# One level of Strassen's algorithm in the second product of five batches

## The chip, the core and the metric

The kernel runs on one core of a Trainium2 chip. TensorE (PE) multiplies; VectorE (DVE), ScalarE (ACT) and GpSimd (POOL) do the elementwise work; SyncE (SP) and the POOL queue issue transfers. The metric is device time in microseconds from a launch on the chip.

## The reference

```python
scores = scale * x @ state.T                  # per batch and head: 512 x 32
a = softmax(scores, -1);   xread = a @ state
scores2 = scale * state @ x.T                 # 32 x 512
a2 = softmax(scores2, -1); sread = a2 @ x
t = concat([xread, sread], axis=2)            # (8, 8, 544, 64)
x2 = t.transpose(0, 2, 1, 3).reshape(4352, 512)
h = x2 @ w_in                                 # 512 -> 2048
g = max(h, 0) + alpha * min(h, 0)
out = g @ w_out                               # 2048 -> 512, float32
```

There are 8 batches of 8 heads, each with 512 tokens and 32 states of width 64. The rows of a batch are its 512 token reads, then its 32 state reads.

## The kernel before

**Stages.** For a batch `b` of token rows, the state times `w_in` is formed first (`state_w_in`, step `m`, and its copy out of PSUM, `mo`), so that the first product needs only the softmax weights: `first` (step `F.b.jc.k`) multiplies the weights of two groups of four heads with `m`, 2 matmuls of 512 columns for each of the 16 blocks `jc` of 128 hidden units. The result `h` (128 hidden units x 512 tokens) lies in PSUM bank `k`. `negative` (step `N`, ACT) writes relu(-h) as float32 to SBUF, and `prelu` (step `G`, DVE), called the gate below, adds it, scaled by 1 - alpha, to `h` and writes `gt` in float16. `second` (step `S.b.q.jc2`) multiplies the gates with `w_out`: for each of 4 token tiles `q`, 16 matmuls of 128 x 128 weights and 512 columns accumulate in one PSUM bank, two to a step. `second_out` (step `O`, ACT or DVE) copies the bank to SBUF and stores it from the SP queue.

**Softmax.** A batch's scores (`sc`) serve both softmaxes. For the token reads: block transpose on DVE (`sb`), maximum (`smax`, DVE), subtraction (`ssh`, here called the shift, POOL), exponential (`sexp`, ACT), sum and reciprocal (`ssum`, DVE), multiplication (`snorm`, the state norm, POOL) and transpose back (`wb`, DVE). For the state reads: maximum and its scaling (`tm`, DVE), exponential (`te`, ACT), reciprocal (`tsum`, DVE), multiplication (`tn`, the token norm, POOL, in place on 128 x 512 float16), a transposing transfer (`tt`, SP queue), 32 narrow matmuls (`rd`) and a cast into `XS` (`rdo`). The state reads of all batches form a ninth batch of 256 rows (`F.8`, `R`, `RO`). The tokens of a batch are loaded from the POOL queue (`lx`) and transposed by a transfer of the SP queue (`xd`).

**Order.** Every step is a token of the text `ORDER` (lines 17 to 102), written out by hand or by a planner, and the kernel issues the steps in that order; each engine takes its own in order, and waits follow from the data and from the buffers. Eight PSUM banks serve everything: a pair `two` for scores and state products and six single ones, whose number is the last part of a token such as `F.2.3.0`. So a first product can go on only when a gate has freed its bank. `L` and `LO` are the last token tile of batch 7 in three pieces of 256, 128 and 128 columns. SBUF buffers with one tag are used in turn: `gt` 2 per block, `neg` 4, `osb` 4, `m` 7.

Of the kernel before, what the change touches and what calls it, by code (L numbers as in the profile page):

```python
# [12 lines left out]
ALU = mybir.AluOpType  # L13
# [28 lines left out]
mo.3.1.a.0 mo.2.2.a.0 S.1.2.7 S.1.0.0.3 mo.3.1.a.1 F.2.3.0 O.1.2.a S.1.0.1 N.2.3 smax.3 F.2.12.5  # L42
N.2.12 G.2.3 F.2.4.2 N.2.4 G.2.12 F.2.2.1 S.1.1.7 F.2.15.0 S.1.0.2 O.1.1.a tm.3 S.1.3.0.5 F.2.0.4
N.2.15 ssh.p.3 S.1.0.3 G.2.4 S.1.3.1 S.1.0.4 F.2.1.2 S.1.3.2 N.2.2 G.2.2 N.2.0 G.2.15 sexp.3 F.2.9.1
G.2.0 S.1.3.3 tsum.2 F.2.6.0 S.1.0.5 N.2.1 G.2.1 S.1.0.6 F.2.13.4 ssum.3 S.1.3.4 N.2.9 te.3.1
F.2.11.2 te.3.0 S.1.3.5 S.1.3.6 N.2.6 G.2.9 G.2.6 F.2.5.1 N.2.13 S.1.3.7 G.2.13 S.1.0.7 N.2.11
G.2.11 N.2.5 O.1.3.a tn.2.0 O.1.0.a F.2.7.0 rd.1.4 G.2.5 m.4.3.2.5 sc.4 m.3.3.1.3 tsum.3 rdo.1.a
mo.4.3.a.1 snorm.p.3 mo.3.3.a.1 wb.3 tn.2.1 N.2.7 mo.3.3.v.0 S.2.1.0.4 lx.5 mo.4.3.v.0 F.3.4.5 G.2.7
S.2.1.1 F.2.8.3 F.2.10.1 N.3.4 S.2.1.2 N.2.8 G.3.4 tt.2 F.3.6.2 N.2.10 G.2.8 G.2.10 F.3.8.0
S.2.0.0.5 N.3.8 F.3.7.3 N.3.6 S.2.1.3 S.2.1.4 N.3.7 F.3.9.1 S.2.0.1 N.3.9 S.2.1.5 tn.3.0 sb.4 tn.3.1  # L50
G.3.7 G.3.8 G.3.9 F.2.14.3 S.2.0.2 S.2.1.6 F.3.13.0 S.2.0.3 F.3.14.1 smax.4 xd.5 S.2.0.4 G.3.6
N.2.14 S.2.0.5 G.2.14 S.2.3.0.2 S.2.3.1 F.3.2.3 S.2.3.2 N.3.14 S.2.3.3 tm.4 N.3.13 S.2.0.6 ssh.p.4
G.3.14 S.2.3.4 S.2.0.7 F.3.1.1 G.3.13 F.3.3.0 sexp.4 te.4.1 ssum.4 te.4.0 N.3.2 S.2.1.7 S.2.3.5
G.3.2 S.2.3.6 tsum.4 S.2.3.7 tt.3 N.3.1 N.3.3 O.2.1.a O.2.0.a G.3.1 m.6.0 G.3.3 O.2.3.a mo.6.0.a.1
m.5.1.3.1 mo.6.0.v.0 snorm.p.4 m.4.2.4.0 rd.2.5 rd.3.2 mo.4.2.a.0 mo.5.1.a.0 rdo.3.a mo.4.2.v.1
rdo.2.v sc.5 m.4.1.4.0 m.5.0.5.3 mo.5.1.v.1 S.2.2.0.2 mo.4.1.a.0 F.3.10.1 tn.4.1 F.3.5.4 tn.4.0
mo.5.0.a.0 mo.4.1.a.1 N.3.10 tm.5 mo.5.0.a.1 S.2.2.1 F.3.11.5 S.2.2.2 F.3.0.0 S.2.2.3 wb.4 N.3.5
S.2.2.4 N.3.11 G.3.10 N.3.0 F.3.12.3 N.3.12 F.4.0.1 S.2.2.5 sb.5 G.3.5 S.2.2.6 lx.6 S.2.2.7 lx.7
te.5.0 F.4.9.4 N.4.0 te.5.1 G.3.11 G.3.12 G.3.0 tsum.5 O.2.2.a F.3.15.5 F.4.6.3 S.3.3.0.0 S.3.3.1
N.4.9 G.4.0 S.3.3.2 S.3.3.3 S.3.3.4 N.3.15 smax.5 S.3.3.5 F.4.5.2 G.3.15 G.4.9 F.4.3.1 tt.4 N.4.6  # L60
tn.5.0 tn.5.1 N.4.3 S.3.3.6 F.4.1.5 G.4.6 G.4.3 N.4.5 tt.5 S.3.0.0.4 G.4.5 S.3.0.1 F.4.4.3 N.4.4
S.3.0.2 ssh.v.5 N.4.1 F.4.2.1 S.3.3.7 S.3.0.3 S.3.0.4 O.3.3.a sexp.5 S.3.0.5 G.4.4 F.4.7.2 G.4.1
S.3.0.6 N.4.7 S.3.1.0.3 S.3.1.1 ssum.5 S.3.1.2 G.4.7 F.4.8.0 F.4.11.5 N.4.8 S.3.0.7 N.4.2 snorm.v.5
N.4.11 S.3.1.3 xd.6 S.3.1.4 S.3.1.5 O.3.0.a S.3.1.6 G.4.2 rd.4.2 G.4.8 rdo.4.a G.4.11 rd.5.1
m.5.3.4.0 rdo.5.a m.5.2.5.2 sc.6 wb.5 tm.6 mo.5.3.a.0 mo.5.2.a.1 S.3.2.0.1 S.3.2.1 F.4.10.4 N.4.10
# [40 lines left out]
def kernel(  # L106
# [47 lines left out]
    def engine(e):  # L154
        return nc.gpsimd if e == "p" else nc.vector
# [4 lines left out]
    def load_x(b):  # L160
# [10 lines left out]
    st0_32 = consts.tile([128, 2, D], F32)  # L171
    x32 = [
        moe.tile([128, 2, 2, 2, D], F32, name=f"x32_{i}", tag="osb", bufs=4) for i in range(2)
    ]
    al32 = consts.tile([32, 128], F32)
# [160 lines left out]
    def score_blocks(b, j=None):  # L336
        if j in (None, 0):
            halved.discard(b) if j is None else halved.add(b)
            live["ts", b] = att.tile([128, 2 * S], F32, name=f"ts_{b}", tag="ts", bufs=2)
            live["mx", b] = att.tile([128, 2 * S // N], F32, name=f"mx_{b}", tag="mx", bufs=2)  # L340
            live["r1", b] = att.tile([128, 2 * S // N], F32, name=f"r1_{b}", tag="r1", bufs=2)
            live["an", b] = att.tile([128, 2 * S], F16, name=f"an_{b}", tag="an", bufs=2)
            live["aT", b] = att.tile([128, 2 * S], F16, name=f"aT_{b}", tag="aT", bufs=2)
# [29 lines left out]
    def state_norm(e, b, j=None):  # L373
        engine(e).tensor_tensor(  # L374
            blocks(cols(live["an", b], j, S)),
            blocks(cols(live["ts", b], j, S)),
            over_blocks(cols(live["r1", b], j, S // N)),
            ALU.mult,
        )

    def weights_back(b, j=None):
        nc.vector.transpose(cols(live["aT", b], j, S), cols(live["an", b], j, S))  # L382
# [275 lines left out]
```

## Time and profile before

| | us |
|---|---|
| three runs | 219.62, 218.71, 219.16 |
| median | 219.16 |
| span of the profiled execution | 217.3 |
| median less span | 1.9 |
| last matmul ends | 214.3 |

The time of the profiled execution itself is not listed apart from the three; the span runs from its first to its last instruction. In the rows below a line of a group has the source line, engine, operation, output <- inputs, shapes and count, then busy time and mean length of one, then idle time before them and what ended it. A line of the timeline has start, length, engine, line, operation and count. Matmuls overlap in the pipeline, so the cost of one in a stream is read from starts, not from its length.

### The profile page before, as it was taken

How to read it: one execution, taken by the hardware profiler on the slowest of the kernel's cores; microseconds unless marked ns; L12 is line 12 of the kernel's file. 1: busy time of each engine (PE TensorE's matmuls, PEld its weight loads, DVE VectorE, ACT ScalarE, POOL GpSimd, SP SyncE). 2: the span in 40 equal slices, each digit the busy share in tenths (PEclk: the TensorE clock that was granted, in tenths of full speed). 3: DMA queues.
4: the chain of work that ended last, by engine and by line, in shares of the span. 5: the costliest groups of instructions: out<-in, count | busy, mean ns of one | idle time of the engine just before them, and what ended most of it. 6: DMA issues, size and time to landing. Idle time of an engine off the chain costs nothing.

```text
span 217.3 us, 4301 instructions
## 1 busy us (share of the span) xinstructions
PE 211.0 (97%) x1692; PEld 104.1 (48%) x1692; DVE 169.2 (78%) x260; ACT 138.0 (63%) x271; POOL 64.8 (30%) x54
## 2 busy tenths in 40 slices
PE   6989999999999999999999999999999999999994
PEld 5763344444444444444454443444455555554553
DVE  1897998899999999798898989989966566665001
ACT  3498995699888748986655768566367336544021
POOL 7589034605238813915000320902200000000000
PEclk9999999999999999999999999999999999999999
DMA  6999999599660875499460432032061011110124
GB/s 148 180 205 207 206 202 160 63 250 168 98 162 3 168 109 113 148 129 163 103 142 0 134 62 98 0 108 41 0 195 51 0 48 51 48 38 10 51 97 145
DMA packets 39316, 23.39 MB, mean 108 GB/s; under 512 B 21872, under 2 KB 35328, under 8 KB 39296
## 3 DMA queue, kind: packets, MB, share of 16 engines
q0 software_dynamic: 12176, 8.36, 26.9%
q1 hardware_dynamic: 26704, 14.43, 26.7%
q10 hardware_dynamic: 416, 0.33, 0.5%
q8 instruction: 13, 0.21, 0.4%
q14 instruction: 7, 0.06, 0.1%
HBM read 17.31 MB, written 8.91 MB: 121 GB/s over the span
## 4 chain that ended last, share of the span: by engine, by line
PE 90%; DVE 6%; DMA 1%; ACT 1%; POOL 0%; issue 0%
PE o L548 49%; PE h L496 24%; PE m_ps L463 3%; PE h L505 3%; PE o L596 3%; DVE gt L536 2%; PE sr_ps L438 2%; PE o L568 2%; DMA st<-in_state_dram 1%; PE sc L313 1%; PE z L232 1%; PE xT_ps L299 1%; DVE aT L382 1%; DVE m L485 1%; DVE r L370 1%; DVE nb L394 1%
## 5 line engine op out<-in xcount | busy, mean ns | idle before, releaser
L548 PE MATMUL o<-w_out_sb,gt 128*128 128x512 f16 x496 | 126.4, 379 | 0.1
L528 ACT ACTIVATE neg<-h 128x512 f32<-128x512 f32 (+1 forms) x144 | 77.4, 580 | 45.2 <-PE h L496 31.4
L536 DVE SCALAR_TENSOR_TENSOR gt<-neg,oma_sb,h 128x512 f16<-128x512 f32 x128 | 89.7, 736 | 15.4 <-ACT neg L528 14.6
L548 PEld LDWEIGHTS <-gt 128*128 128x128 f16 x496 | 47.3, 98 | 54.9 <-issue 3.7
L496 PE MATMUL h<-aT,m 128*128 128x512 f16 x250 | 69.2, 379 | 0.3 <-DVE gt L536 0.3
L496 PEld LDWEIGHTS <-m 128*128 128x128 f16 x250 | 24.2, 98 | 29.7 <-issue 1.6
L419 POOL TENSOR_SCALAR e<-e,r 128x512 f16<-128x512 f16 x16 | 25.0, 1568 | 25.2 <-DVE r L415 20.6
L485 ACT CAST m<-m_ps 128x512 f16<-128x512 f32 x50 | 27.9, 603 | 3.7 <-PE m_ps L463 2.0
L360 POOL TENSOR_TENSOR ts<-ts,mx 128x1024 f32<-128x1024 f32 (+1 forms) x8 | 13.6, 1698 | 43.6 <-DVE mx L354 43.6
L586 ACT COPY osb<-o 128x512 f32<-128x512 f32 x22 | 12.8, 591 | 16.4 <-PE o L548 16.4
L374 POOL TENSOR_TENSOR an<-ts,r 128x1024 f16<-128x1024 f32 (+1 forms) x7 | 11.7, 1667 | 18.1 <-DVE r L371 18.0
L405 ACT ACTIVATE e<-sc,nb 128x512 f16<-128x512 f32 x16 | 11.1, 697 | 1.5 <-issue 1.5
L463 PE MATMUL m_ps<-w_in_sb,stT 64*32 64x512 f16 x256 | 11.7, 383 | 0.1
L536 DVE SCALAR_TENSOR_TENSOR gs<-neg,oma_sb,h 128x256 f16<-128x256 f32 x16 | 7.5, 476 | 5.1 <-ACT neg L528 5.1
L370 DVE TENSOR_REDUCE r<-ts 128x32 f32<-128x1024 f32 (+1 forms) x9 | 9.8, 1093 | 1.3 <-ACT ts L366 1.3
L485 DVE CAST m<-m_ps 128x512 f16<-128x512 f32 x14 | 9.3, 684 | 1.6 <-ACT m L485 1.4
L382 DVE STREAM_TRANSPOSE aT<-an 128x1024 f16<-128x1024 f16 (+1 forms) x9 | 10.0, 1114 | 0.5 <-POOL an L374 0.4
L354 DVE TENSOR_REDUCE mx<-ts 128x32 f32<-128x1024 f32 (+1 forms) x9 | 9.9, 1096 | 0.1
L394 DVE TENSOR_REDUCE nb<-sc 128x2 f32<-128x1024 f32 x8 | 9.7, 1212 | 0.1
L232 PE MATMUL z<-zero 128*128 128x128 f16 x76 | 7.6, 263 | 1.9 <-DVE zero L226 1.1
L606 DVE COPY osr<-o 128x512 f32<-128x512 f32 x1 | 0.7, 692 | 11.3 <-PE o L596 11.3
L505 PE MATMUL h<-XS,w_in_sb 128*128 128x256 f16 x64 | 9.4, 273 | 0.0
(55 smaller groups left out, 130.9 us busy)
## 6 DMA issues: line engine op xcount, KB each, us to landing
out_dram<-osb SPq DMA_DIRECT2D x29, 256.0 KB, 2.3
xg<-in_x_dram POOLq DMA_DIRECT2D x7, 512.0 KB, 7.5
w_in_sb<-in_moe_w_in_dram POOLq DMA_DIRECT2D x4, 512.0 KB, 11.6
w_out_sb<-in_moe_w_out_dram POOLq DMA_DIRECT2D x4, 512.0 KB, 12.8
out_dram<-osb SPq DMA_DIRECT2D x5, 128.0 KB, 2.0
out_dram<-osr SPq DMA_DIRECT2D x2, 256.0 KB, 2.5
x<-in_x_dram SPq DMA_DIRECT2D x1, 256.0 KB, 3.7
x<-in_x_dram ACTq DMA_DIRECT2D x1, 256.0 KB, 3.9
```

The source lines that it names most:

```text
L360: engine(e).tensor_tensor(ts, ts, over_blocks(cols(live["mx", b], j, S // N)), ALU.subtract)
L370: nc.vector.tensor_reduce(r1, blocks(cols(live["ts", b], j, S)), AX.X, ALU.add)
L382: nc.vector.transpose(cols(live["aT", b], j, S), cols(live["an", b], j, S))
L419: nc.gpsimd.tensor_scalar_mul(e2, e2, live["r2", b][:, g : g + 1])
L463: nc.tensor.matmul(t[N * k : N * (k + 1), :], st_head(b, h)[64 * r : 64 * r + 64, :], w_in_sb[64 * r : 64 * r + 64, c, 512 * f : 512 * (f ...
L485: copier(e)(m_tile(b)[:, f, g, :], live["mp", b, f][g])
L496: nc.tensor.matmul(h.rearrange("p (r j s) -> p r j s", r=2, j=2), ms[b][:, f, g, 128 * j : 128 * (j + 1)], weights(b, g), start=(g == 0), ...
L505: nc.tensor.matmul(h, w_in_sb[:, c, 128 * jc : 128 * (jc + 1)], XS[:, c].rearrange("p q n b -> p (q n b)"), start=(c == 0), stop=(c == n_c ...
L528: nc.scalar.activation(neg, h, RELU, bias=0.0, scale=-1.0)
L536: nc.vector.scalar_tensor_tensor(gt, negs.pop((b, jc)), oma_sb[:, jc : jc + 1], h, ALU.mult, ALU.add)
L548: nc.tensor.matmul(outs[b, q], gts[b, jc][:, 128 * q : 128 * (q + 1)], w_out_sb[:, jc, :], start=(jc == 0), stop=(jc == n_jc - 1),)
L586: copier(e)(osb, t)
```

## The change

The second product of batches 2 to 6 is no longer made by `second` and `second_out`. Let A be the gates of a batch (512 tokens x 2048 hidden units) and B the matrix `w_out` (2048 x 512), each cut in 2 x 2 blocks: tokens in halves of 256, hidden units in halves of 8 blocks, output columns in halves of 256. The form with seven products and fifteen additions (Winograd's) is used:

- `weight_sum` (steps `T`, POOL, eight pieces in all): four matrices `ws` from the blocks of B, once: B12 - B11, B22 - ws0, B22 - B12, B21 - ws1.
- `token_sum_of` (steps `A.b.i.grp`, POOL, eight per batch): s1 = A21 + A22, s3 = A11 - A21, s2 = A22 - s3, s4 = A12 - s2, each in two groups of four blocks, 128 x 4 x 256 in float16.
- `product` (steps `P.b.p.c`): seven products, each of 8 blocks x 2 token tiles in matmuls of 256 columns, four to a step. Products 1, 6, 7 and 4 accumulate in one bank, 5 and 3 in a second, 2 in a third.
- `product_out` (steps `Q`): the bank of product 1 is copied behind product 1 (`p1`) and behind product 6 (`u`), product 5's behind product 5 (`p5`); c11 = p1 + product 2; c22 = p5 + the first bank behind product 7; c12 = u + the second bank behind product 3; c21 = the first bank behind product 4. Copies are on ACT (one `u` on DVE), the three additions of a batch on DVE. Each quarter, 256 tokens x 256 columns, is stored from SP.

The gates of four blocks now share a tile (`gp`, two groups, 2 buffers each), and those of the ninth batch take a buffer of tag `m`. Tags and counts change: `m` 5 buffers, `osb` 5, and some constants share `neg`. Of the softmax steps behind the cut, the token norms of batches 2 to 7 go from POOL to DVE, and the two state norms and one shift that DVE had go to POOL. Behind `mo.3.1.a.1` every step of all engines is in a new order; ahead of it none is.

```diff
@@ order, from where it differs (two stretches)
-mo.3.1.a.0 mo.2.2.a.0 S.1.2.7 S.1.0.0.3 mo.3.1.a.1 F.2.3.0 O.1.2.a S.1.0.1 N.2.3 smax.3 F.2.12.5
+mo.3.1.a.0 mo.2.2.a.0 S.1.2.7 S.1.0.0.3 mo.3.1.a.1 T.0.0.p T.0.1.p tsum.2 tm.3 rd.1.0 O.1.2.a
+S.1.0.1 rdo.1.a T.1.0.p F.2.0.2 tn.2.0.v te.3.1 tn.2.1.v S.1.0.2 smax.3 tt.2 F.2.1.5 N.2.0 S.1.0.3
...
+sb.5 F.4.2.0 mo.5.0.a.0 P.3.5.0.2 mo.5.0.a.1 F.4.3.5 tm.5 N.4.2 P.3.5.1 N.4.3 A.3.2.0.p F.4.8.1
+P.3.5.2 G.4.2 N.4.8 F.4.9.4 te.5.1 G.4.3 P.3.5.3 F.4.10.0 N.4.9 G.4.8 A.3.2.1.p P.3.6.0 Q.3.p5.a
+G.4.9 P.3.2.0.5 N.4.10 P.3.6.1 smax.5 te.5.0 F.4.11.1 lx.6 P.3.6.2 N.4.11 G.4.10 m.5.1 ssh.p.5
+P.3.6.3 mo.5.1.a.0 G.4.11 P.3.2.1 mo.5.1.a.1 tsum.5 F.4.4.4 Q.3.u.v P.3.2.2 tn.5.0.v N.4.4 A.3.4.0.p
+P.3.7.0 tn.5.1.v sexp.5 tt.5 G.4.4 P.3.2.3 F.4.5.0 Q.3.c11.v P.3.7.1 N.4.5 ssum.5 F.4.6.1 A.3.4.1.p
...
-    def token_norm(b, g):
+    def token_norm(b, g, e="p"):
         e2 = live["e2", b][:, g, :, :]
-        nc.gpsimd.tensor_scalar_mul(e2, e2, live["r2", b][:, g : g + 1])
+        r2 = live["r2", b][:, g : g + 1]
...
+            engine(e).tensor_scalar_mul(e2, e2, r2)
...
-            gt = moe.tile(list(h.shape), F16, name=f"gt_{b}_{jc}", tag=f"gt{jc}", bufs=2)
+            grp = jc % 8 // 4
+            if (b, grp) not in gps:
+                gps[b, grp] = moe.tile(
+                    [128, 2, 4, S], F16, name=f"gp_{b}_{grp}", tag=f"gp{grp}", bufs=2
+                )
+            gt = gps[b, grp][:, jc // 8, jc % 4, :]
...
+    def token_sum_of(b, i, grp, e):
+        t = sums[b, i, grp] = moe.tile(
+            [128, 4, half_s], F16, name=f"s{i}_{b}_{grp}", tag=f"s_{grp}", bufs=3
+        )
+        gp = gps[b, grp]
+        a11, a12, a21, a22 = (
+            gp[:, k, :, half_s * r : half_s * (r + 1)] for r in range(2) for k in range(2)
+        )
+        x, y, op = {
+            1: (a21, a22, ALU.add),
+            2: (a22, sums.get((b, 3, grp)), ALU.subtract),
+            3: (a11, a21, ALU.subtract),
+            4: (a12, sums.get((b, 2, grp)), ALU.subtract),
+        }[i]
+        engine(e).tensor_tensor(t, x, y, op)
+
+    chain_of = {1: 1, 6: 1, 7: 1, 4: 1, 2: 0, 5: 2, 3: 2}
+
+    def product(b, p, c, k=None):
+        chain = b, chain_of[p]
+        opens = p in (1, 2, 5)
+        if opens and c == 0:
+            chains[chain] = single(k, f"p{p}_{b}", [128, 2, half_d], F32)
+        for i in (2 * c, 2 * c + 1):
+            for t in range(2):
...
+                nc.tensor.matmul(
+                    chains[chain][:, t, :],
+                    lhs,
+                    rhs[:, i, :],
+                    start=(opens and i == 0 and t == 0),
+                    stop=(i == half_k - 1),
+                    skip_group_check=True,
+                )
...
+    def product_out(b, name, e):
+        if name in ("p1", "p5", "u"):
+            t = parts[b, name] = moe.tile(
+                [128, 2, half_d], F32, name=f"{name}_{b}", tag="osb", bufs=5
+            )
+            copier(e)(t, chains[b, 2 if name == "p5" else 1])
+            return
+        osb = moe.tile([128, 2, half_d], F32, name=f"{name}_{b}", tag="osb", bufs=5)
+        if name == "c21":
+            copier(e)(osb, chains.pop((b, 1)))
+        else:
+            chain, part = {"c11": (0, "p1"), "c12": (2, "u"), "c22": (1, "p5")}[name]
+            nc.vector.tensor_tensor(osb, parts.pop((b, part)), chains[b, chain], ALU.add)
+        nc.sync.dma_start(block_rows(b, *blocks_of[name]), osb)
```

More of the change, by code (lines that the diff above doesn't have):

```diff
@@ L170 @@
     n_j = (B * H * N - n0) // 128
-    st0_32 = consts.tile([128, 2, D], F32)
+    st0_32 = moe.tile([128, 2, D], F32, name="st0_32", tag="neg", bufs=4)
     x32 = [
-        moe.tile([128, 2, 2, 2, D], F32, name=f"x32_{i}", tag="osb", bufs=4) for i in range(2)
+        moe.tile([128, 2, 2, 2, D], F32, name=f"x32_{i}", tag="osb", bufs=5) for i in range(2)
     ]
-    al32 = consts.tile([32, 128], F32)
+    al32 = moe.tile([32, 128], F32, name="al32", tag="neg", bufs=4)
     nc.vector.memset(al32, 0.0)
@@ L373, in state_norm @@
     def state_norm(e, b, j=None):
+        if ("an", b) not in live:
+            live["an", b] = att.tile([128, 2 * S], F16, name=f"an_{b}", tag="an", bufs=2)
         engine(e).tensor_tensor(
@@ L381, in weights_back @@
     def weights_back(b, j=None):
+        if ("aT", b) not in live:
+            live["aT", b] = att.tile([128, 2 * S], F16, name=f"aT_{b}", tag="aT", bufs=2)
         nc.vector.transpose(cols(live["aT", b], j, S), cols(live["an", b], j, S))
@@ L528, in negative, with reads_tile @@
         nc.scalar.activation(neg, h, RELU, bias=0.0, scale=-1.0)
+    def reads_tile():
+        if "gs" not in live:
+            live["gs"] = moe.tile([128, n_jc, B * N], F16, name="gs", tag="m", bufs=5)
+        return live["gs"]
     def prelu(b, jc):
@@ L554, in second, with w_block, weight_sum @@
             )
+    half_k, half_d, half_s = n_jc // 2, d_model // 2, S // 2
+    ws = {}
+    sums = {}
+    chains = {}
+    parts = {}
+    def w_block(k, d):
+        return w_out_sb[:, half_k * k : half_k * (k + 1), half_d * d : half_d * (d + 1)]
+    def weight_sum(i, part, e):
+        if i not in ws:
+            ws[i] = consts.tile([128, half_k, half_d], F16, name=f"ws_{i}")
+        b11, b12, b21, b22 = (w_block(k, d) for k in range(2) for d in range(2))
+        x, y = ((b12, b11), (b22, ws.get(0)), (b22, b12), (b21, ws.get(1)))[i]
+        at = slice(4 * part, 4 * part + 4)
+        engine(e).tensor_tensor(ws[i][:, at, :], x[:, at, :], y[:, at, :], ALU.subtract)
@@ L584, in second_out @@
         t = outs.pop((b, q))
-        osb = moe.tile([128, d_model], F32, name=f"osb_{b}_{q}", tag="osb", bufs=4)
+        osb = moe.tile([128, d_model], F32, name=f"osb_{b}_{q}", tag="osb", bufs=5)
         copier(e)(osb, t)
@@ L604, in second_reads_out @@
     def second_reads_out(q, e):
-        osb = moe.tile([128, d_model], F32, name=f"osr_{q}", tag="osb", bufs=4)
+        osb = moe.tile([128, d_model], F32, name=f"osr_{q}", tag="osb", bufs=5)
         copier(e)(osb, outs.pop((B, q)))
```

146 lines of the change are left out of this document (81 added, 65 removed).

## The prediction

> **What bounds the kernel now.** I read the page first, for the busy shares and the chain that ended last.
>
> ```profile
> span 217.3 us, 4301 instructions
> PE 211.0 (97%) x1692; PEld 104.1 (48%) x1692; DVE 169.2 (78%) x260; ACT 138.0 (63%) x271; POOL 64.8 (30%) x54
> ...
> PE 90%; DVE 6%; DMA 1%; ACT 1%; POOL 0%; issue 0%
> PE o L548 49%; PE h L496 24%; PE m_ps L463 3%; PE h L505 3%; PE o L596 3%; DVE gt L536 2%; PE sr_ps L438 2%; PE o L568 2%; DMA st<-in_state_dram 1%; PE sc L313 1%; PE z L232 1%; PE xT_ps L299 1%; DVE aT L382 1%; DVE m L485 1%; DVE r L370 1%; DVE nb L394 1%
> ```
>
> TensorE (PE) carries 90% of the chain, and half of the chain is the second product, line 548, which the change rewrites for five batches. Busy shares are averages, so next I cut the span where the two orders part. That is at the matmul which opens the third batch (58.35); the second cut is at the first matmul of batch 7.
>
> ```profile
> 58.35 0.59 PE L496 MATMUL h<-aT,m 128*128 128x512 f16 x2
> ```
>
> ```profile
> 58.35:163.50 105.15, 105.15 (x856) 48.48 (x855) 95.35 (x137) 73.01 (x143) 34.76 (x22) 1.00 0.46 99
> 163.50:217.40 53.90, 50.82 (x299) 27.78 (x297) 24.32 (x43) 20.64 (x45) 0.00 (x0) 1.00 0.15 54
> ```
>
> The columns after the length are PE, weight loads, DVE (VectorE), ACT (ScalarE), POOL (GpSimd), clock, DMA share and GB/s. In the first stretch PE is busy for all of its 105.15 us at full clock, while DVE fills 95.35, ACT 73.01 and POOL 34.76. The list of PE's waits agrees: the last and only one on the elementwise work is small.
>
> ```profile
> PE h L496 <- DVE gt L536: 0.3, 1, 0.3
> ```
>
> So matmul time taken out behind 58.35 shortens the span one for one, until another engine fills its stretch. Ten microseconds of free DVE time is the smallest cushion.
>
> **The matmuls.** Pieces of the chain (start, length, count) give what one matmul costs in a stream, each with its own weight load; the first two are two state reads, 0.56 each, and one batch's scores, 0.4.
>
> ```profile
> 89.26 1.12 PE sr_ps L438 x64
> 90.38 0.41 PE sc L313 x16
> ...
> 110.40 2.16 PE o L548 x10
> ...
> 180.95 0.87 PE h L505 x8
> ...
> 213.42 0.91 PE o L568 x16
> ```
>
> A 512-column matmul costs 2.16/10 = 0.216 us, a 256-column one 0.87/8 = 0.109, a 128-column one 0.91/16 = 0.057. A batch had 64 of the first kind, 13.82 us. Seven products of 8 blocks times 2 token tiles are 112 of the second kind, 12.21 us. Five batches save 5 x 1.61 = **8.1 us**. That weight loads come twice as often costs nothing extra here, because the 128-column row already has them four times as often.
>
> The new order also splits the narrow matmuls (state times weights, scores, state reads) into more groups. Behind 58.35 I count 7 uninterrupted groups in the old order and 15 in the new. A group has an entry and an exit cost:
>
> ```profile
> 120.87 1.03 PE L496 MATMUL h<-aT,m 128*128 128x512 f16 x4
> 121.83 0.41 PE L463 MATMUL m_ps<-w_in_sb,stT 64*32 64x512 f16 x8
> 122.17 0.60 PE L548 MATMUL o<-w_out_sb,gt 128*128 128x512 f16 x2
> ...
> 130.81 0.59 PE L548 MATMUL o<-w_out_sb,gt 128*128 128x512 f16 x2
> 131.34 0.62 PE L463 MATMUL m_ps<-w_in_sb,stT 64*32 64x512 f16 x16
> 131.90 1.90 PE L548 MATMUL o<-w_out_sb,gt 128*128 128x512 f16 x8
> ```
>
> The last wide matmul before the first group starts at 120.87 + 3 x 0.216 = 121.52 and the next at 122.17: 0.65, less its own 0.216 leaves 0.43 for 8 narrow matmuls. The second group, from 131.03 to 131.90, leaves 0.65 for 16. So eight cost 0.22 and a group 0.21. Eight more groups add **1.7 us**.
>
> At the end the last three pieces are now all copied by ACT, close together, instead of one.
>
> ```profile
> 214.35 0.27 ACT L579 COPY osb<-o 128x128 f32<-128x128 f32 x1 [0.26 <-PE o L568]
> 214.64 0.33 SPq L580 DMA_DIRECT2D out_dram<-osb  x1
> ```
>
> Another such copy may stand behind the last matmul, and its store behind another store: 0 to 0.6, I take **0.3 us**.
>
> **DVE.** Up to the first matmul of batch 7 the new order gives it 3 more gates (line 536), 12 additions of a PSUM chain to an SBUF part, one PSUM copy, 12 token norms taken from POOL and 4 more state-read casts; it takes away 6 output copies, 4 casts of the state product, two state norms and one shift.
>
> ```profile
> 5.12 0.43 DVE L197 CAST xg<-x 128x512 f16<-128x512 f32 x1 [0.99 <-DMA x<-in_x_dram]
> ...
> 89.63 1.29 DVE L485 CAST m<-m_ps 128x512 f16<-128x512 f32 x2 [1.17 <-ACT m L485]
> 90.84 0.43 DVE L449 CAST XS<-sr_ps 128x128 f16<-128x128 f32 x1
> 91.08 0.71 DVE L485 CAST m<-m_ps 128x512 f16<-128x512 f32 x1
> ...
> 95.98 2.68 DVE L536 SCALAR_TENSOR_TENSOR gt<-neg,oma_sb,h 128x512 f16<-128x512 f32 x4
> ...
> 109.79 1.22 DVE L374 TENSOR_TENSOR an<-ts,r 128x1024 f16<-128x1024 f32 x1
> ...
> 119.60 0.68 DVE L586 COPY osb<-o 128x512 f32<-128x512 f32 x1
> ```
>
> Four gates take 2.68, so 0.66 each with the overlap; an addition has the same operands but for its f32 output, so 0.66 too. Copies and casts take 0.6, the read cast 0.24 (90.84 to 91.08), a norm or shift of 1024 some 1.14. The token norm on DVE is not in the trace: at least the 0.17 of a tiny scalar operation (below), at most the 0.66 of a gate; the nearest row is the SBUF cast of 512 at 0.43, with f32 input, so I take 0.3. Added: 3 x 0.66 + 12 x 0.66 + 0.6 + 12 x 0.3 + 4 x 0.24 = 15.1. Removed: 6 x 0.6 + 4 x 0.6 + 3 x 1.14 = 9.4. DVE rises from 95.35 to 101.0 us.
>
> PE in the same stretch loses 143 old steps of 0.432 (61.8) and gains 17 of these (7.3), 113 new steps of 4 x 0.109 (49.3), 3 first-product steps (1.3) and 7 groups (1.5); one state read, 0.56, falls behind the cut. That is 105.15 - 3.0 = 102.2 us. **DVE then fills 101 of 102**, where it filled 95 of 105. The order is written so that first products alternate with the new products, and three PSUM banks let PE run a little ahead of DVE. Still, little slack is left for a DVE that waits for ACT or PE. I charge PE **2 us** of stalls: none if the order holds as the old one did, 6 if each of the five batches loses 1.2.
>
> ACT gets 7 casts, 3 negatives and 14 copies, and loses 9 copies and 4 read casts, all near 0.6: about 80 of 102, and it is hidden.
>
> **POOL.** It loses 12 token norms and gains 8 weight differences, 40 block sums, two norms and a shift.
>
> ```profile
> L419 POOL TENSOR_SCALAR e<-e,r 128x512 f16<-128x512 f16 x16 | 25.0, 1568 | 25.2 <-DVE r L415 20.6 <-ACT ts L366 4.4
> L360 POOL TENSOR_TENSOR ts<-ts,mx 128x1024 f32<-128x1024 f32 x6 | 11.5, 1914 | 40.6 <-DVE mx L354 40.6
> L374 POOL TENSOR_TENSOR an<-ts,r 128x1024 f16<-128x1024 f32 x5 | 9.6, 1914 | 17.5 <-DVE r L371 17.5
> L162 POOL DMA_DIRECT2D xg<-in_x_dram x7 | 6.6, 937 | 0.9 <-PE sr_ps L438 0.9
> ```
>
> A block sum is 1024 elements from two f16 inputs, which no row has. With f32 inputs it is 1.91 whether the output is f32 or f16; by the f16 scalar row it would be 2 x 1.57 = 3.14. Same operation and size are nearer, so 1.91. A batch of eight sums, a shift, a norm and an x load then holds POOL 10 x 1.91 + 0.94 = 20.0 us. PE's batch is 32 x 0.216 for a first product, 12.2 for a second, 4 x 0.22 + 0.4 + 0.56 for the narrow ones and 0.7 for their three or four groups, 21.6 us. It fits, with little slack, and the eight weight differences, 15.3 us, must fit the opening. They can start early:
>
> ```profile
> 53.93 1.91 POOL L374 TENSOR_TENSOR an<-ts,r 128x1024 f16<-128x1024 f32 x1 [2.40 <-DVE r L371]
> 59.77 1.91 POOL L360 TENSOR_TENSOR ts<-ts,mx 128x1024 f32<-128x1024 f32 x1 [3.93 <-DVE mx L354]
> ```
>
> POOL is free from 55.84, and a shift queued behind four differences starts at 63.5, near where the new order has it. The x loads are now queued behind sums too:
>
> ```profile
> xg<-in_x_dram POOLq DMA_DIRECT2D x7, 512.0 KB, 7.5
> out_dram<-osb SPq DMA_DIRECT2D x29, 256.0 KB, 2.3
> ```
>
> The order has a load some 17 us ahead of the scores that need it; 7.5 to land and the transposing DMA leave about 5. Output stores on SP are as many and as large, in half rows; the 2.3 us to land is covered by five buffers for seven uses a batch. Fewer buffers for the state products and the reordered tile tags cost nothing while fewer than five are alive at once.
>
> **The sum.** 217.3 - 8.1 + 1.7 + 0.3 + 2.0 = 213.2 us of span. The three runs shown have a median of 219.16, 1.9 us above this span; which of them was profiled is not listed. So **215.1 us**; without stalls 213.1.
>
> **Rivals.** *DVE and POOL block each other* (slower). The trace shows it once:
>
> ```profile
> 91.37 1.84 POOL L162 DMA_DIRECT2D xg<-in_x_dram  x2
> ```
>
> ```profile
> 92.95 0.26 DVE L397 TENSOR_SCALAR nb<-nb 128x2 f32<-128x2 f32 x1
> ...
> 115.79 0.17 DVE L397 TENSOR_SCALAR nb<-nb 128x2 f32<-128x2 f32 x1
> ```
>
> With POOL idle this operation takes 0.17; at 92.95 it took 0.26 and ended at 93.21, as POOL's instruction did. The 12 token norms move to DVE and have the same kind, a scalar operation from SBUF to SBUF, and POOL will nearly always be in a 1.91 us sum. If each pair of norms and each of the 5 maxima's scalings waits half a sum, that is 11 x 0.96 = 10.5 us; DVE comes to 111.5 of 102.2, and the time to 213.1 + 9.3 = **222**. Behind a blocked norm queue the gates, and behind these, through the three banks, PE's first products. It eats the whole gain from 6.1 + 1.2 = 7.3 us of waits on, 0.66 each. Against it: the one wait seen was 0.09, and where DVE has slack at that moment it costs nothing. The Trainium skill (SBUF — State Buffer, Who interferes with whom) says it as a rule: a VectorE instruction in a two-port mode, which scalar operations and casts between SBUF tiles can enter, takes an interface that it shares with GpSimd for its whole length, and whoever comes second waits it out. By that rule the time is near the 222 above. The row agrees for a descriptor-writing instruction; no row shows it against a sum.
>
> *f16 sums cost POOL more than f32 ones.* POOL's batch passes PE's 21.6 at (21.6 - 4.8)/8 = 2.10 us a sum; the gain of 6.1 over five batches is gone at 2.10 + 6.1/40 = 2.25. At 3.14 each batch takes 29.9, 8.3 more, near **255**; the products wait for the sums, and all of PE's work queues behind them. For it: the f16 row; against: f16 output was free.
>
> *The PSUM chain waits.* Products 6, 7 and 4 add onto the bank of product 1, each behind a copy or addition that reads it. In batch 3 the copy between products 6 and 7 is on DVE, with 1.3 us of other matmuls as cover against 0.68 and the matmul's drain. If the reader stands behind one more gate, 0.4 is lost; 15 such waits make **219**.
>
> *Weight loads bind at 256 columns.* At 13.82/112 = 0.123 us a matmul the saving is nil: **223**. The 0.057 row speaks against it.
>
> **How the numbers follow.** The forecast, PE still the bound with small stalls, 0.50, with 213.0 to 217.5 of its own; blocking 0.20; dear sums 0.15; chain waits 0.10; weight loads 0.05. Half a per cent, 1.1 us, is what a measurement of this kernel can tell from no change, so faster is below 218.1 and slower above 220.3. Faster: 0.49 + 0.03 + 0.02 + 0.04 = 0.58. Within: 0.01 + 0.05 + 0.03 + 0.04 = 0.13. Slower: 0.12 + 0.10 + 0.02 + 0.05 = 0.29. From 212.8 to 223.0 lie the forecast, the chain waits, most of the blocking and the mildest dear sums, 0.80.
>
> **What would show it.** Right: 256-column rows of lines for products at 0.109 each, PE idle for 1 to 4 us behind 58 us in total and spread out, sums of 1.9, DVE at 95% or more up to batch 7. Blocking: token norms on DVE of 1 us and more that end with a POOL sum. Dear sums: their mean above 2.1 and PE waiting for POOL. Chain waits: PE products waiting for ACT or DVE readers. I am wrong if PE waits over 6 us behind 58, or if products cost more than 0.12 each.

## The result, and the profile after

| | before | after |
|---|---|---|
| median, us | 219.16 | 238.79 |
| lowest to highest, us | 218.71 to 219.62 | 238.56 to 239.69 |
| span of the profiled execution, us | 217.3 | 237.9 |
| last matmul ends, us | 214.3 | 234.2 |

The ratio is 1.0908, with an interval of 1.088 to 1.0937: the kernel is 19.6 us slower. The page of the changed kernel, its busy shares, its slices and its chain by engine:

```profile
span 237.9 us, 4897 instructions
...
PE 213.1 (90%) x1932; PEld 128.2 (54%) x1932; DVE 193.3 (81%) x271; ACT 147.6 (62%) x284; POOL 152.5 (64%) x93
...
PEclk9999999999958999999999996799979999999999
...
PE 55%; DVE 34%; DMA 3%; ACT 3%; issue 2%; POOL 1%; ACTq 0%; POOLq 0%
```

DVE, 6% of the chain before, now carries 34% of it, and the PE clock, which the throttle had left alone, dips in three places (the digits under 9 in the row PEclk). The stretch behind 58 us in the view by windows (columns as before), and three stretches in which the clock was halved:

```profile
58.35:165.00 106.65, 94.10 (x907) 57.91 (x907) 101.70 (x130) 69.83 (x132) 95.30 (x49) 0.94 0.42 87
```

```profile
66.20:73.00 6.80, 6.50 (x45) 2.73 (x45) 6.76 (x10) 3.10 (x5) 5.60 (x4) 0.50 0.32 60
144.70:151.50 6.80, 5.36 (x21) 3.04 (x21) 5.20 (x8) 2.14 (x3) 2.43 (x2) 0.50 0.20 39
175.40:178.80 3.40, 3.40 (x16) 2.13 (x15) 2.79 (x5) 0.60 (x1) 0.00 (x0) 0.51 0.40 77
```

PE no longer fills its stretch, and what it waits for behind 58 us is almost all one thing, the gate (line 557 now), which frees its banks:

```profile
PE h L507 <- DVE gp L557: 14.8, 9, 5.2
PE h L507 <- DVE aT L389: 0.9, 2, 0.5
PE m_ps L474 <- DVE gp L557: 0.5, 1, 0.5
PE sr_ps L449 <- DVE gp L557: 0.3, 1, 0.3
```

The gates are late because of what stands ahead of them on DVE. Three groups of the page (busy time, mean ns), and the same token norm as a source line with its shortest, median and longest case; behind it the scaling of a maximum, seen by its tile behind 58 us:

```profile
L608 POOL TENSOR_TENSOR s<-gp 128x1024 f16<-128x1024 f16 x20 | 42.2, 2129 | 9.3 <-PE p L630 5.4
...
L608 POOL TENSOR_TENSOR s<-gp,s 128x1024 f16<-128x1024 f16 x20 | 42.5, 2140 | 0.5 <-PE p L630 0.5
...
L430 DVE TENSOR_SCALAR e<-e,r 128x512 f16<-128x512 f16 x12 | 22.4, 1902 | 0.1
```

```profile
L430 DVE TENSOR_SCALAR e<-e,r x12: 339/2119/6000, 59.9 to 172.2; 128x512 f16<-128x512 f16 x12
```

```profile
L404 DVE TENSOR_SCALAR nb<-nb x5: 393/1270/1883, 59.6 to 165.2; 128x2 f32<-128x2 f32 x5
```

The token norm has a shortest case of 0.34 us and a mean of 1.90, so the twelve stand 12 x (1.902 - 0.339) = 18.8 us on DVE without doing more. The five scalings took 393, 1427, 1270, 473 and 1883 ns where the kernel before has 169: 4.6 us more. Together DVE loses 23.4 us. The longest case shows how. The timelines of DVE, POOL and PE around 140 us (start, length, engine, line, operation, count, and in brackets idle time before it and what ended it):

```profile
139.17 6.26 DVE L430 TENSOR_SCALAR e<-e,r 128x512 f16<-128x512 f16 x2
145.35 2.05 DVE L557 SCALAR_TENSOR_TENSOR gp<-neg,oma_sb,h 128x512 f16<-128x512 f32 x3
```

```profile
138.94 2.14 POOL L608 TENSOR_TENSOR s<-gp,s 128x1024 f16<-128x1024 f16 x1
141.03 1.91 POOL L363 TENSOR_TENSOR ts<-ts,mx 128x1024 f32<-128x1024 f32 x1
142.90 2.11 POOL L608 TENSOR_TENSOR s<-gp,s 128x1024 f16<-128x1024 f16 x1
147.54 2.13 POOL L608 TENSOR_TENSOR s<-gp 128x1024 f16<-128x1024 f16 x1 [2.54 <-DVE gp L557]
```

```profile
140.37 0.60 PE L630 MATMUL p<-w_out_sb,gp 128*128 128x256 f16 x4
146.14 1.01 PE L507 MATMUL h<-aT,m 128*128 128x512 f16 x2 [5.17 <-DVE gp L557]
146.94 1.06 PE L630 MATMUL p<-w_out_sb,gp 128*128 128x256 f16 x4
147.80 1.06 PE L630 MATMUL p<-ws,s 128*128 128x256 f16 x4
```

The first norm of the pair begins at 139.17, just after a block sum on POOL, and ends at 145.17, 0.16 us after POOL's third instruction in a row (142.90 + 2.11 = 145.01). The second norm, with POOL idle, takes 0.34. Behind them the three gates, and behind these PE, idle for 5.17 us. Then the second loss: PE comes back at half clock. Groups of four matmuls of 256 columns start 0.86 us apart (146.94, 147.80) instead of 4 x 0.109 = 0.436, until 151.5.

Against the span that I predicted without stalls, 217.3 - 8.1 + 1.7 + 0.3 = 211.2, the execution is 26.7 us longer. Gaps on PE longer than 0.1 us make up 16.8 of it behind 58 us. The five over 0.5 us, 2.64, 1.50, 0.64, 5.17 and 3.51, all end behind a norm or scaling that stood. In the three stretches at half clock, matmuls of 512 and 256 columns start farther apart than the 0.216 and 0.109 of full clock; that makes 2.4, 2.6 and 1.7, together 6.7. The other 3.2 was not taken apart; the refilling behind each gap and the narrow matmuls at half clock are in it.

### The profile page after: what moved, and what is told of

It is laid out like the page before. It is cut to its first block, busy times and chain, and to the rows that moved or that the text cites. A ratio compares the mean times of both kernels' runs of the same rounds, so it can differ in the third digit from the quotient of the medians.

```text
span 237.9 us, 4897 instructions
## 1 busy us (share of the span) xinstructions
PE 213.1 (90%) x1932; PEld 128.2 (54%) x1932; DVE 193.3 (81%) x271; ACT 147.6 (62%) x284; POOL 152.5 (64%) x93
## 4 chain that ended last, share of the span: by engine, by line
PE 55%; DVE 34%; DMA 3%; ACT 3%; issue 2%; POOL 1%; ACTq 0%; POOLq 0%
PE h L507 15%; PE p L630 14%; PE o L569 13%; DVE gp L557 11%; DVE e L430 9%; DMA w_in_sb<-in_moe_w_in_dram 3%; PE h L516 3%; PE o L700 3%; DVE ts L349 3%; DVE mx L357 2%; DVE nb L401 2%; DVE nb L404 2%; PE m_ps L474 2%; PE sr_ps L449 2%; DVE aT L389 2%
## 5 line engine op out<-in xcount | busy, mean ns | idle before, releaser
L557 DVE SCALAR_TENSOR_TENSOR gp<-neg,oma_sb,h 128x512 f16<-128x512 f32 x128 | 89.8, 735 | 9.5 <-ACT neg L539 7.8
L608 POOL TENSOR_TENSOR s<-gp 128x1024 f16<-128x1024 f16 x20 | 42.2, 2129 | 9.3 <-PE p L630 5.4
L569 PE MATMUL o<-w_out_sb,gp 128*128 128x512 f16 x176 | 47.5, 388 | 0.1
L608 POOL TENSOR_TENSOR s<-gp,s 128x1024 f16<-128x1024 f16 x20 | 42.5, 2140 | 0.5 <-PE p L630 0.5
L630 PEld LDWEIGHTS <-s 128*128 128x128 f16 x320 | 31.7, 100 | 16.1 <-issue 1.6
L630 PE MATMUL p<-ws,s 128*128 128x256 f16 x240 | 35.9, 280 | 0.2
L630 PEld LDWEIGHTS <-gp 128*128 128x128 f16 x240 | 23.9, 101 | 10.4 <-issue 0.8
L569 PEld LDWEIGHTS <-gp 128*128 128x128 f16 x176 | 16.9, 99 | 20.8 <-issue 3.9
L630 PE MATMUL p<-w_out_sb,gp 128*128 128x256 f16 x160 | 25.9, 287 | 0.0
L430 DVE TENSOR_SCALAR e<-e,r 128x512 f16<-128x512 f16 x12 | 22.4, 1902 | 0.1
L630 PE MATMUL p<-ws,gp 128*128 128x256 f16 x80 | 12.0, 273 | 0.0
```

The source lines that it names most:

```text
L430: engine(e).tensor_scalar_mul(e2, e2, r2)
L557: nc.vector.scalar_tensor_tensor(gt, negs.pop((b, jc)), oma_sb[:, jc : jc + 1], h, ALU.mult, ALU.add)
L569: nc.tensor.matmul(outs[b, q], gts[b, jc][:, 128 * q : 128 * (q + 1)], w_out_sb[:, jc, :], start=(jc == 0), stop=(jc == n_jc - 1),)
L608: engine(e).tensor_tensor(t, x, y, op)
L630: nc.tensor.matmul(chains[chain][:, t, :], lhs, rhs[:, i, :], start=(opens and i == 0 and t == 0), stop=(i == half_k - 1), skip_group_chec ...
```

## The experiments

Four explanations stood against each other. That DVE's scalar operations wait for POOL on something the two share (the lock). That a token norm is simply dear on DVE, 1.9 us of its own. That the block sums, at 2.13 and not 1.91, make POOL the bound. And that the new order has waits of its own. In the table a single figure is one timed run; the ratio stands against the kernel before on the same chip.

| run | edit to the changed kernel | us | ratio, interval |
|---|---|---|---|
| e1 | token norms on ACT | 226.63 | 1.034, 1.0305 to 1.0375 |
| e4 | (kernel before) token norms on DVE | 219.6 | one run, 219.37 before |
| e3 | block sums a quarter as long | 223.26 | one run |
| e5 | token norms on DVE in another form | 227.1 | 1.0355, 1.0301 to 1.0408 |
| e2 | norms and scalings on ACT | 221.56 | 1.0107, 1.0086 to 1.0129 |
| e8 | norms and scalings in the other form | 221.88 | 1.0135, 1.0102 to 1.0167 |
| e6 | e2, three weight sums early | 222.49 | 1.0149, 1.0111 to 1.0187 |
| e9 | e2, sums a quarter as long | 221.44 | one run |
| e7 | token norms back on POOL | 245.6 | one run |
| e10 | e1, one gap filled | 226.3 | 1.0359, 1.0292 to 1.0426 |
| e12 | no lock, and a new order | 214.06 | 0.9767, 0.9743 to 0.979 |

### Is the norm dear, or is it blocked? (e4, e3, e1)

First the norm alone: the kernel before, where POOL is idle two thirds of the time, with its norms on DVE.

```diff
-        nc.gpsimd.tensor_scalar_mul(e2, e2, live["r2", b][:, g : g + 1])
+        (nc.vector if b > 1 else nc.gpsimd).tensor_scalar_mul(e2, e2, live["r2", b][:, g : g + 1])
```

> The kernel before with its 12 token norms of batches 2 to 7 on DVE and nothing else changed: POOL is mostly idle there. Theory A: most norms meet an idle POOL and take 0.25 to 0.45 us, DVE grows by about 4 us and has the room, 218.5 to 220.5. Theory D (1.9 us of its own): DVE grows by 22 us, 225 to 235.

The same source line in that run, shortest, median and longest:

```profile
L419 DVE TENSOR_SCALAR e<-e,r x12: 303/346/689, 69.3 to 154.7; 128x512 f16<-128x512 f16 x12
```

So 0.35 us is the price; 0.69 and a 0.41 came where POOL wrote an x load. The time, 219.6, didn't move. Next, sums a quarter as long in the changed kernel (their text says what is left out):

```diff
-        engine(e).tensor_tensor(t, x, y, op)
+        engine(e).tensor_tensor(t[:, :1, :], x[:, :1, :], y[:, :1, :], op)
-                    lhs = lhs[:, i % 4, 128 * t : 128 * (t + 1)]
+                    lhs = lhs[:, 0, 128 * t : 128 * (t + 1)]
```

> The changed kernel with every block sum on POOL cut to a quarter (one of its four blocks is summed and used four times, so three quarters of the sums are left out). Theory A: a norm waits for at most one short instruction, so the norms take 0.3 to 0.7 us each, PE hardly waits, 212 to 217. Theory D (a norm on DVE costs 1.9 of its own): the norms stay at 1.9 us, DVE stays over-full, above 225.

The norms behind 90 us, where quarter sums run, and the sums:

```profile
L430 DVE TENSOR_SCALAR e<-e,r x8: 345/758/2032, 91.4 to 159.0; 128x512 f16<-128x512 f16 x8
```

```profile
L608 POOL TENSOR_TENSOR s<-gp,s x20: 657/670/794, 80.2 to 177.5; 128x256 f16<-128x256 f16 x20
```

With 0.67 us sums the norm's median is 0.76: 0.35 and a wait of 0.41, and it ends 0.15 us after a sum. Two took 2.03: each began soon after a shift of 1.91 us and outlasted it. The norm's length is that of POOL's instruction beside it. That it costs 1.9 of its own is out. The time, 223.26, is in neither of the two expected ranges: the edit leaves the weight sums whole, and behind the norms that stood beside them PE still has a gap of 2.64 us at 63 us, and 6.8 us at half clock from 65.5 on. Last, the norms taken off DVE:

```diff
-S.1.0.1 rdo.1.a T.1.0.p F.2.0.2 tn.2.0.v te.3.1 tn.2.1.v S.1.0.2 smax.3 tt.2 F.2.1.5 N.2.0 S.1.0.3
+S.1.0.1 rdo.1.a T.1.0.p F.2.0.2 tn.2.0.a te.3.1 tn.2.1.a S.1.0.2 smax.3 tt.2 F.2.1.5 N.2.0 S.1.0.3
...
```

> The changed kernel with the 12 token norms of batches 2 to 7 on ACT instead of DVE, at the same places of the order. Theory A (blocking): the norms took 22.8 us of DVE because each waited for POOL's running instruction; on ACT they take 0.6 to 0.7 each and wait for no one, the long PE gaps (2.6, 5.2 and 3.5 us) and with them the half-speed clock go, and the time is 214 to 221. The 5 scalings of the maxima stay on DVE and still wait, 3 to 5 us in all. Theory B (dear sums: POOL is simply over-full with sums at 2.13 instead of 1.91): PE goes on waiting for gates and sums, and the time stays above 230.

226.63: 12.2 us came back, and the time is still above the 214 to 221 expected. What stood longest in this run is a scaling, two numbers a partition:

```profile
L404 DVE TENSOR_SCALAR nb<-nb x8: 168/246/5920, 12.3 to 157.8; 128x2 f32<-128x2 f32 x8
```

```profile
130.91 0.40 PE L474 MATMUL m_ps<-w_in_sb,stT 64*32 64x512 f16 x4
135.30 0.62 PE L474 MATMUL m_ps<-w_in_sb,stT 64*32 64x512 f16 x4 [3.99 <-DVE gp L557]
```

One scaling of 0.17 us of work stood for 5.92, through the rest of a sum, another sum, an x load and a third sum, and cost PE a gap of 3.99 us and a stretch at half clock behind it.

### Taking the lock away without moving work (e5, e8)

A form of the same multiplication that also writes a sum per partition, on the same engine and at the same place of the order. The Trainium skill (SBUF — State Buffer, Who interferes with whom) excepts exactly this form from those that enter a two-port mode.

```diff
-            engine(e).tensor_scalar_mul(e2, e2, r2)
+            junk = att.tile([128, 1], F32, name=f"junk_{b}_{g}", tag="junk", bufs=2)
...
+                nc.vector.tensor_scalar(e2, e2, r2, 0.0, ALU.mult, ALU.add, accum_out=junk)
```

> The changed kernel with the 12 token norms still on DVE, at the same places, but in the form that also writes the sum of its output (a throwaway number). Theory A (blocking by a shared interface in a two-port mode): this form does not use the second port, so each norm takes about 0.65 us whatever POOL runs, against 1.90 on average, and the time is 215 to 223. Theory B (dear sums): above 230. Theory C (any DVE instruction between SBUF tiles is held up by POOL's sums): the norms stay near 1.9 us and the time near 239.

```profile
L432 DVE TENSOR_SCALAR_CACHE_REDUCE e<-e,r x12: 734/742/747, 61.2 to 163.1; 128x512 f16<-128x512 f16 x12
```

Twelve norms within 13 ns of each other, whatever POOL does: the trace agrees with the Trainium skill. It is slower than a free norm (0.74 and 0.08 for reading the sum, against 0.35), and far cheaper than a blocked one. The scalings, still in the old form, stood for up to 5.96 us, and the time is e1's, 227.1, again above the expected 215 to 223. With the scaling in the new form too:

```diff
-        nc.vector.tensor_scalar_mul(nb, nb, -scale)
+        nc.vector.tensor_scalar(nb, nb, -scale, 0.0, ALU.mult, ALU.add, accum_out=junk)
```

> The changed kernel with its order and engines as they are; only the 12 norms and the 8 scalings of the maxima take the form that also writes an accumulator. Theory A: norms 0.74 us and scalings about 0.25 whatever POOL runs, no PE wait above 1.5 us, no half clock, and the time is 220 to 223, as with both on ACT (221.56): the 16 to 19 us below 238.8 are then the price of the second port alone. If it stays above 225, moving work to ACT did something that the port does not explain.

The scalings are then 0.155 each (and 0.083 for reading the sum), and PE's largest waits behind 58 us are these:

```profile
L405 DVE TENSOR_SCALAR_CACHE_REDUCE nb<-nb x5: 155/155/156, 60.8 to 152.4; 128x2 f32<-128x2 f32 x5
```

```profile
PE h L512 <- DVE aT L389: 2.3, 3, 1.5
PE p L635 <- POOL s L613: 1.9, 5, 1.0
PE h L512 <- DVE c L662: 1.0, 1, 1.0
```

Nothing but the form of two instructions differs from the changed kernel, in engine and order both, and 238.79 becomes 221.88. The lock, with the half clock that its gaps brought, is 16.9 us of the 19.6, or somewhat more, since the new form is itself longer than a free norm. No wait for a gate over 0.3 us is left, and no stretch at half clock behind 58.

### What is left, 8.5 us above the plan without stalls (e2, e6, e9)

The same without a lock in another way: e1's edit, and the scalings on ACT too:

```diff
-        nc.vector.tensor_scalar_mul(nb, nb, -scale)
+        nc.scalar.mul(nb, nb, -scale)
```

> The run with the norms on ACT had 226.63 us and kept 5 scalings on DVE that waited up to 5.9 us for three POOL instructions in a row; one 4.0 us wait of PE and 6.8 us at half clock lay right behind it. Here the scaling of the maxima is on ACT too, so no DVE instruction uses the second port behind 58 us. Theory A (blocking is the whole cause): the 4.0 us wait and the half clock go, 217 to 221. Theory B (sums at 2.13 and a full DVE are the rest of the cause): PE still waits some 4 us in many places, 222 to 225.

221.56, as with e8, between the two expected ranges. PE's waits in it are many and of different kinds; the four largest entries:

```profile
PE m_ps L474 <- ACT e L412: 1.3, 1, 1.3
PE h L507 <- DVE gp L557: 1.3, 4, 0.4
PE h L507 <- DVE aT L389: 1.2, 3, 0.5
PE p L630 <- POOL s L608: 1.1, 3, 0.5
```

Two suspects were tried on it. POOL starts late, because the first weight sums stand behind 58 us; three of them moved ahead:

```diff
-te.2.0 F.1.9.4 G.1.6 N.1.14 G.1.4 smax.2 rd.0.3 m.2.3 F.1.11.5 N.1.9 mo.2.3.a.1 G.1.9 F.1.8.0 tn.1.1
+te.2.0 F.1.9.4 G.1.6 N.1.14 G.1.4 smax.2 rd.0.3 m.2.3 F.1.11.5 N.1.9 mo.2.3.a.1 G.1.9 F.1.8.0 tn.1.1 T.0.0.p T.0.1.p T.1.0.p
...
-mo.3.1.a.0 mo.2.2.a.0 S.1.2.7 S.1.0.0.3 mo.3.1.a.1 T.0.0.p T.0.1.p tsum.2 tm.3 rd.1.0 O.1.2.a
+mo.3.1.a.0 mo.2.2.a.0 S.1.2.7 S.1.0.0.3 mo.3.1.a.1  tsum.2 tm.3 rd.1.0 O.1.2.a
-S.1.0.1 rdo.1.a T.1.0.p F.2.0.2 tn.2.0.a te.3.1 tn.2.1.a S.1.0.2 smax.3 tt.2 F.2.1.5 N.2.0 S.1.0.3
+S.1.0.1 rdo.1.a  F.2.0.2 tn.2.0.a te.3.1 tn.2.1.a S.1.0.2 smax.3 tt.2 F.2.1.5 N.2.0 S.1.0.3
```

> The last run's kernel with three of the eight weight differences moved ahead on POOL, into its 6.9 us of idle time at 41.6 us. POOL is then 6.4 us ahead at 58 us. If late sums hold PE (theory B), this takes 1 to 4 us off the last run; if POOL is no longer on the path, it changes less than 0.5.

222.49, no gain. And the price of a sum, with e3's edit made in e2:

> Norms and scalings on ACT as in the first run of this call, and every block sum cut to a quarter (three quarters of the sums left out). What is then left is the matmul plan itself. If the plan of the prediction was right, PE never waits behind 58 us and the time is 212 to 214.5; what it is above that is neither blocking nor the price of the sums.

221.44 where I had expected 212 to 214.5: a miss, and the one that taught most. In the windows of that run POOL is busy for half of the stretch, and PE for hardly more of it than in e2, 100.96:

```profile
58.35:165.00 106.65, 101.22 (x1005) 64.89 (x1004) 91.40 (x131) 85.06 (x169) 58.56 (x56) 1.00 0.46 92
```

So it isn't the sums. What was left to suspect was the order: steps on four queues that wait for each other a little at a time.

### Undoing the move (e7) and filling a gap (e10)

The norms back on POOL, as they were before, all else as changed:

```diff
-S.1.0.1 rdo.1.a T.1.0.p F.2.0.2 tn.2.0.v te.3.1 tn.2.1.v S.1.0.2 smax.3 tt.2 F.2.1.5 N.2.0 S.1.0.3
+S.1.0.1 rdo.1.a T.1.0.p F.2.0.2 tn.2.0.p te.3.1 tn.2.1.p S.1.0.2 smax.3 tt.2 F.2.1.5 N.2.0 S.1.0.3
...
```

> The changed kernel with the 12 token norms back on POOL, as in the kernel before: that part of the change undone, nothing else. Theory A (blocking): no long DVE waits, but POOL gets 12 x 1.57 = 19 us on top of sums at 2.13, about 8 x 2.13 + 2 x 1.91 + 0.94 + 3.1 = 24.9 us a batch against PE's 21.6, so POOL sets the pace: 226 to 234, and PE waits for sums and POOL's other work. If it were under 222, the norms should never have moved.

245.6, worse than expected and than the changed kernel. The scalings and PE's waits behind 58 us:

```profile
L404 DVE TENSOR_SCALAR nb<-nb x8: 169/490/7060, 12.1 to 170.0; 128x2 f32<-128x2 f32 x8
```

```profile
PE m_ps L474 <- DVE gp L557: 8.5, 2, 4.5
PE p L630 <- POOL s L608: 6.3, 8, 1.7
PE sr_ps L449 <- DMA e2T<-e: 4.0, 1, 4.0
```

The norms queue behind sums on POOL and the sums behind norms, so PE waits for sums and for the transfer of a normalized tile; and POOL, busy for 103.14 of the 106.65 us behind 58.35, lets three scalings stand for 4.1, 7.1 and 5.9 us. The lock isn't a matter of the norms alone. In this order the norms cost more on POOL than on DVE; how much of that is the scalings' waits this run doesn't separate, so it doesn't show that the norms had to move.

The half clock by itself: e1 has one long gap, and 60 matmuls of zeros in it keep PE busy.

```diff
-P.4.5.2 G.5.2 N.5.8 P.4.6.0 te.6.1 G.5.3 P.4.5.3 P.4.6.1 te.6.0 G.5.8 lx.7 m.6.1.2.1 Q.4.p5.a smax.6
+P.4.5.2 G.5.2 N.5.8 P.4.6.0 te.6.1 G.5.3 P.4.5.3 P.4.6.1 te.6.0 G.5.8 lx.7 Z.2.60 m.6.1.2.1 Q.4.p5.a smax.6
```

> The run with the norms on ACT (226.63, ratio 1.034) had one 4.0 us gap of PE at 131.3 us, and its clock was at half from 134.0 to 140.9. Here 60 matmuls of zeros (60 x 0.056 = 3.4 us) stand in that gap, in a free PSUM bank; the gap's cause stays. If the gap is what halves the clock, it stays at full speed and the time falls by the 2 to 3 us that half speed took, to 223.5 to 225. If the clock falls for another reason, nothing changes.

```profile
130.64 3.51 PE L237 MATMUL z<-zero 128*128 128x128 f16 x60
134.21 0.40 PE L474 MATMUL m_ps<-w_in_sb,stT 64*32 64x512 f16 x4
135.13 0.40 PE L474 MATMUL m_ps<-w_in_sb,stT 64*32 64x512 f16 x4 [0.52 <-DVE gp L557]
```

In the profiled execution the clock stayed whole (mean 0.999 against 0.985) and the span fell from 224.8 to 223.7. The median, 226.3, is within e1's: two executions at a mean clock of 0.999 took 225.4 and 225.5, but two at 0.990 and 0.985 took 227.1 and 228.5. Where the clock fell in those two isn't known, since the only trace is that of an execution at 0.999. On the time this run decides nothing.

### Without the lock, in another order (e12)

Scalings and one norm on DVE in the form of e5, eleven norms on ACT, and all steps behind 58 us laid out anew with the durations of these traces. The sums, the products and their number are those of the changed kernel; three weight sums stand ahead of 58 us, product 6 often goes ahead of 5, 23 copies and casts change sides between ACT and DVE, and many steps use another PSUM bank. From two places of its order:

```diff
-mo.3.1.a.0 mo.2.2.a.0 S.1.2.7 S.1.0.0.3 mo.3.1.a.1 T.0.0.p T.0.1.p tsum.2 tm.3 rd.1.0 O.1.2.a
-S.1.0.1 rdo.1.a T.1.0.p F.2.0.2 tn.2.0.v te.3.1 tn.2.1.v S.1.0.2 smax.3 tt.2 F.2.1.5 N.2.0 S.1.0.3
...
+m.2.2.5.3 mo.2.2.a.1 m.3.1.0.2 sc.3 wb.2 sb.3 S.1.2.6 mo.3.1.a.0 mo.2.2.a.0 S.1.2.7 tsum.2 S.1.0.0.3
+F.2.0.0 O.1.2.a mo.3.1.a.1 tm.3 F.2.1.5 T.2.1.p tn.2.0.a tn.2.1.a T.1.1.p smax.3 T.2.0.p S.1.0.1 rd.1.2
...
+F.3.3.3 G.3.1 P.2.6.1 A.2.3.1.p mo.4.3.a.0 P.2.5.0.4 rdo.3.a P.2.5.1 tm.4 mo.4.1.a.0 F.3.2.2 A.2.1.1.p
```

> The same arithmetic with the scalings of the maxima and one norm in the one-port form on DVE and the other norms on ACT, and with all steps behind 58 us in another order, made for sums of 2.11 us, norms of 0.73 and gates, negatives and matmuls as the runs show them. If the matmul plan is sound (8.1 us less in the products) and what remained at 221.56 was only small waits of the old order, these go and the time is 213 to 216, faster than the kernel before. If the waits come from DVE or POOL being full, it stays at 219 or above.

214.06: 2.3% faster than the kernel before. The page, the window and all of PE's waits behind 58 us:

```profile
span 212.0 us, 4874 instructions
...
PE 204.4 (96%) x1932; PEld 126.5 (60%) x1932; DVE 171.0 (81%) x276; ACT 146.7 (69%) x288; POOL 151.8 (72%) x93
```

```profile
58.35:165.00 106.65, 106.20 (x1082) 70.16 (x1081) 99.52 (x151) 86.72 (x170) 105.05 (x54) 1.00 0.46 97
```

```profile
PE sr_ps L451 <- DMA e2T<-e: 0.4, 1, 0.4
```

PE is busy for 106.20 of 106.65 us, with DVE at 99.52 and POOL at 105.05. Neither fill is a bound by itself. Since e2 and e8 have no lock either, the 7.5 and 7.8 us between them and this run come with the new layout: its order, banks and engines together. Small waits are most of it: gaps on PE over 0.1 us add up to 6.0 us behind 58 us in e2 (13 gaps) and 6.2 in e8 (12), and to 0.4 here. Which part of the layout removed which of them was not taken apart further.

## Why the prediction was wrong

**The matmuls were right.** 211.2 us of span without stalls, against 212.0 in the one run without them, of which 0.4 is its one wait. The terms hold one by one, so it isn't luck: matmuls of the products start 0.109 apart at full clock in the traces of the changed kernel and of e12, and both have 15 narrow groups behind 58 us. The end came out at 3.5 to 3.7 us behind the last matmul, where it had been 3.0, and I had added 0.3. Of the rivals, weight loads that bind are out by that 0.109. Waits in the PSUM chain are out too: in the changed kernel and in e8 no product waits for a reader of its bank, and e12 has no such wait either.

**The step that failed is the token norm on DVE, taken at 0.3 us.** The 0.3 was right for a free one (0.35 in e4). In place it cost 1.90, twelve times. With it went the 5 scalings, which I left at their old price in the sum. The sign I had named for blocking, norms of 1 us and more that end with a POOL sum, is what the trace shows, and PE waits 16.8 us behind 58 where I had set 6 as the mark of being wrong. The reason stood in the prediction as a rival, and I weighed its one row wrongly: a wait of 0.09 behind an x load told nothing of the length of a wait. That scaling began just before POOL's instruction was over. The row's message was that it *ended with POOL's instruction*; the length is then whatever is left of it, up to a whole sum or, as it turned out, several.

**The rival's price was too low in three places.** I let each pair of norms wait once; in four of the six batches both waited. I let a wait be half a sum, 0.96; 15 waits made 23.4 us, 1.56 each, because a norm that is queued right behind another meets a fresh sum from its start. And I turned DVE's excess into time one for one and stopped there, at 222. PE's gaps became long enough to halve its clock, 6.7 us which no case of mine had. The Trainium skill (SBUF — State Buffer, Who interferes with whom), which the prediction cited, has whoever is second blocked for the whole of the other's instruction; these runs bear that out, and in six cases the wait outlasts three or four of them.

**The stalls, taken at 2 and at most 6 us, were too low as well.** Without the lock this order still cost 221.88 - 214.06 = 7.8 us more than e12's. My argument was that DVE at 101 of 102 us is tight. Full engines aren't what costs: of 106.65 us, DVE and POOL fill 99.52 and 105.05 in e12, and 99.66 and 106.58 in e8; e9 fills 91.40 and 58.56 and is no faster than e2. That leaves the layout, which step stands behind which, and no share shows that.

**The sums at 1.91 were mis-sized, without effect of their own.** They took 2.13, just above the 2.10 at which I let POOL's batch outgrow PE's. By that rival shorter sums had to save time; e9, one run with sums of 0.67 and no lock, took 221.44 against e2's 221.56. With the lock their length sets the length of the waits.

## What to carry to other kernels

Before work moves onto an engine, list the instructions there that share something with the engine that will be busy beside it, the tiny ones too; if one row ends with the other's instruction, price it at that instruction's whole length. A gap on PE has two prices, the gap and the clock behind it. Judge a new order with the lock removed before judging the idea: here the same seven products are 9% slower or 2% faster.

## What had not been expected of the hardware

**A blocked DVE instruction can lose to several POOL instructions in a row.** In the five traces with such cases (after, e1, e5, e7, e10) the six waits of 5.6 us and more passed three or four POOL instructions, and each ended only when POOL then had nothing ready for 2.5 to 3.3 us. At 139.17 POOL's pause came because it waited for a gate queued behind the blocked norm. Most other waits ended after one instruction, with POOL going on at once. What decides which, no run tells.

**A gap of 2.64 us on PE was enough for half clock.** Behind 58 us the traces have nine gaps from 2.64 to 5.17 us (after, e1, e3, e5, e7). At each the clock fell, during the gap or at most 1.5 us behind it, to half for 3.4 or 6.8 us. Behind gaps of up to 1.80 us it didn't fall; no run has a gap between 1.80 and 2.64. The Trainium skill (TensorE: Matmul & The Clock Gate, Why this matters for your kernels) asks for no gap over some 3 us; here 2.64 was already too long.

**A sum of 1024 elements of two float16 inputs, one or both read in four pieces, took 2.13 us on POOL**, against 1.91 for a shift or norm whose float32 input is in one piece and whose second input has one value for each 32 elements. Which of these differences makes the 0.22 wasn't tried.
